# Row order of x, the first unit's y copied in place, the last token with its unit, later loads and a separate last gate in a fused recurrence and MLP

## The chip, the cores and the metric

One core of a Trainium2 chip runs the whole program. The metric is the device time of one execution in microseconds. All arithmetic is float32.

## The reference

A gated linear recurrence over 768 tokens for 4 batches and 8 heads of 48 channels, then an MLP with a quick GELU on its output:

```python
f = 1.0 / (1.0 + np.exp(-f_logit))                     # [4, 8, 768, 48]
for t in range(S):
    state = f[:, :, t, :, None] * state + np.einsum('bhd,bhe->bhde', k[:, :, t], v[:, :, t])
    y[:, :, t] = np.einsum('bhd,bhde->bhe', q[:, :, t], state)
x = y.transpose(0, 2, 1, 3).reshape(3072, 384)
h = x @ w_in                                           # w_in [384, 2048]
out = (h * (1.0 / (1.0 + np.exp(-1.702 * h)))) @ w_out  # w_out [2048, 384]
```

## The kernel before

**Units.** The 3072 tokens are 12 units of 256 (three to a batch; `NALL = 12`, `N_FILL = 3`). Each unit goes through an attention part (`attention(n)`) and an MLP part, and TensorE interleaves the MLP of earlier units (`fill`) with the attention of the next (`merge`). The order on TensorE and POOL is written out by hand throughout. Up to `fill_order.close()`, that is through the opening and `merge(1)` to `merge(3)`, the order on all engines is written by hand; behind that ScalarE, VectorE and SP are ordered by the framework. SP issues nearly all transfers, in one list; an instruction at its head that waits holds back what is behind it.

**Attention of a unit.** f, q and k are loaded into `raw` (`load_raw`), turned so that channels lie on partitions (`turn`: by TensorE through PSUM tiles t for units 0 to 2, by VectorE later), and worked through in six doubling levels: ScalarE sets keys aside (`Kc`, L494), TensorE makes scores (`sc`, L425), VectorE multiplies X by the gates (`promote`, L519 and L523) and moves scores into A (`evacuate`; L475 on ScalarE for the last level). The gates are products of f on POOL (`begin_gates`, L416): each level halves the row `tot`, and the last level goes to a tile of its own, `D64`, for units above 4. The states st of the four chunks are computed by VectorE from pd and the last gate (L667, L668). Tokens of the second half are kept in reverse order, so the rows of v for one half are reversed (`reverse_v`, a VectorE shuffle, L309). TensorE adds A times v (`add`, L534) and the states times q (L689) into y, a PSUM tile.

**From y to x.** y has 64 partitions for each of two groups of heads, of which 48 are used, and four pairs of heads a (`NP = 4`). ScalarE copies y to yT (L701, eight copies, 48 partitions by 256 columns) and SP moves it to xT, which has three tiles of 128 rows (`NK = 3`): three of the four pairs lie in rows 0 to 95, the fourth pair is split over rows 96 to 127 (`to_x`, L740 and L745; six transfers a unit). The rows of w_in are loaded in the same order. `half(0)` and `half(1)` do this for each half of the partitions. The last token's y (q is used one token late) is computed apart, behind the last unit (L724, L730, six more transfers).

**MLP.** Units 0 to 3 compute h directly from xT and w_in (L1087). From unit 4 on h is computed by 20 products in place of 24, on sums E of blocks of x that POOL makes (`sums_of_x`, L955) and sums of w_in blocks. The products of a unit follow a list, `WHOLE`, or for the last unit, which has two more columns and works in two column groups, `HALVES`: each item names a product, its group and a lane. Lanes 0 to 3 are PSUM tiles of their own; lanes 4 and 5 are the halves of one tile (h_y in the profile), 6 and 7 of another (h_sc). An item -1 emits four of the 16 matmuls that are still to do for the unit before (the last two products, o_Y and o_Z). The product with w_out takes seven products instead of eight (`mlp_o7`, L856).

**Weights.** 16 pairs of blocks of w_in and w_out are loaded as bits (`fetch_weights`, L210), rounded by ScalarE and VectorE (`begin_pair`, `convert`, L228 to L233) and written to w_in and w_out during units 0 to 3.

**Opening.** `opening()` loads unit 0, turns it, runs its six levels, turns its k (`turn_k`), evacuates, turns q and k of unit 1 and computes the states and y of unit 0. Just ahead of the states' end one element of y is copied onto itself by ScalarE (`seen`, L654).

Of the kernel before, what the change touches and what calls it, by code (L numbers as in the profile page):

```python
# [23 lines left out]
def kernel(  # L24
# [134 lines left out]
    def query(n, f):  # L159

        return ((2, 3), (4, 5) if n < N_FILL else (0, 5))[n % 2][f]

    q_end = const.tile([P, NP], F32, name="q_end")
    nc.gpsimd.memset(q_end, 0.0)

# [2 lines left out]
    w_in = const.tile([P, NK, DFF], F32, name="w_in")  # L168
    w_out = const.tile([P, NFF, DM], F32, name="w_out")
    k_toks = [tc.dram_tile([2, G, P // 32, 32 * NP], F32, name=f"k_tok{j}") for j in range(2)]  # L170
    D2, DR = 2 * D, P - 2 * D
    assert NP == NK + 1 and NK * DR == D2

    NGR = NFF // FG

# [2 lines left out]
    for r in range(NGR):  # L178
        ffs = range(r * FG, (r + 1) * FG)
        for ff in ffs[::2]:  # L180
            f = slice(ff * P, (ff + 2) * P)
            pairs.append((w_in[:, :, f], [
                (lambda t: t[:D2], moe_w_in[0:NK * D2, f].rearrange("(c p) f -> p c f", c=NK)),
                (lambda t: t[D2:], moe_w_in[NK * D2:DM, f].rearrange("(c p) f -> p c f", c=NK)),
            ]))
        for ff in ffs[::2]:
            pairs.append((w_out[:, ff:ff + 2, :], [
                (lambda t: t[:], moe_w_out[ff * P:(ff + 2) * P, :].rearrange("(c p) f -> p c f", c=2))]))
# [100 lines left out]
    def load_v(n):  # L289


        if n >= NALL:
            return
        b, s0 = n // NU, n % NU * U
        vts[n] = ld.tile([P, 2, DM], F32, tag="vt", name=f"vt_{n}", bufs=2)
        vrs[n] = ld.tile([P, DM], F32, tag="vr", name=f"vr_{n}", bufs=1)
        nc.sync.dma_start(
            out=vts[n][:, 1].rearrange("p (h d) -> p h d", h=H), in_=v[b, :, s0:s0 + HALF, :].rearrange("h p d -> p h d")
        )
        for i in range(4):  # L300
            t0 = s0 + U - 32 * (i + 1)
            nc.sync.dma_start(
                out=vrs[n][32 * i:32 * (i + 1)].rearrange("p (h d) -> p h d", h=H),
                in_=v[b, :, t0:t0 + 32, :].rearrange("h p d -> p h d"),
            )

    def reverse_v(n):

        nc.vector.stream_shuffle(vts[n][:, 0], vrs[n], list(range(31, -1, -1)))  # L309

    def rows(h):
# [7 lines left out]
    def attention(n):  # L319
# [86 lines left out]

        def begin_gates():
            t["tot"], off = att.tile([P, NA], F32, tag="tot", name=f"tot_{n}"), 0
            for m in LEV:
                nb = NA // (2 * m)  # L410
                t2 = t["tms"][-1].rearrange("p (n two) -> p n two", two=2)
                tn = t["tot"][:, off:off + nb]

                if m == LEV[-1] and n > N_FILL + 1:
                    tn = att.tile([P, nb], F32, tag="D64", name=f"D64_{n}", bufs=2)
                nc.gpsimd.tensor_tensor(tn, t2[:, :, 0], t2[:, :, 1], ALU.mult)  # L416
                t["tms"].append(tn)
                off += nb
# [212 lines left out]
        def _():  # L631
# [40 lines left out]
        def _():  # L672
# [4 lines left out]
            for cs in ((1, 0), (2, 3)):  # L677
                for a in range(NP):
                    for c in cs:
                        g, f = CHUNK[c]  # L680
                        w = HS
                        if t["before"][c] is None:
                            if not n:
                                continue
                            w = 1
                        for h in range(2):
                            state = t["before"][c][rows(h), a] if w > 1 else t["ahead"][rows(h), NC - 1, a]
                            x = a * HALF + g * HS
                            nc.tensor.matmul(  # L689
                                py[columns(h, g), g, a, f, :w], lhsT=state, rhs=X[rows(h), query(n, f), x:x + w],  # L690
                                start=False, stop=True, skip_group_check=True,
                            )
            yT = att.tile([P, NP, NG, G], F32, tag="kn", name=f"yT_{n}", bufs=1)
            xT = mlp.tile([P, NK, width(n)], F32, tag="xT", name=f"xT_{n}", bufs=3)
            if width(n) > U:
                nc.gpsimd.memset(xT[:, :, U + 1:], 0.0)
            def half(h):
                for f in (1, 0):
                    for g in range(NG):
                        at, step = (g * HS, 1) if f else (U - 1 - g * HS, -1)  # L700
                        nc.scalar.copy(view(yT[rows(h)], at, [[U, NP], [step, HS]]), py[columns(h, g), g, :, f, :])  # L701
# [14 lines left out]
            xTs[n] = xT  # L716
            if n == 0:
                fetch_weights()
            if n == NALL - 1:

                pl = ps.tile([P, NP], F32, tag="sc", name="y_last")
                for a in range(NP):
                    for h in range(2):
                        nc.tensor.matmul(  # L724
                            pl[rows(h), a:a + 1], lhsT=last["st"][rows(h), NC - 1, a], rhs=q_end[rows(h), a:a + 1],
                            start=True, stop=True,
                        )
                yl = att.tile([P, NP], F32, tag="q_last", name="yT_last", bufs=1)
                for h in range(2):
                    nc.scalar.copy(yl[rows(h)], pl[rows(h)])  # L730
                yl = yl.rearrange("p (a g t) -> p a g t", g=1, t=1)
                to_x(lambda h: (yl[rows(h), :NK], lambda r, d: yl[r:r + d, NK]), xT[:, :, U:U + 1], 1)
            if n > N_FILL:
                sums_of_x(n)

        def to_x(y, x, ng, hs=range(2)):

            for h in hs:
                most, rest = y(h)
                nc.sync.dma_start(out=x[h * D:(h + 1) * D].rearrange("p c (g t) -> p c g t", g=ng), in_=most)  # L740
                at = 0
                while at < D:
                    c, p = (h * D + at) // DR, (h * D + at) % DR
                    w = min(D - at, DR - p)
                    nc.sync.dma_start(  # L745
                        out=x[D2 + p:D2 + p + w, c].rearrange("p (g t) -> p g t", g=ng), in_=rest(h * HS + at, w)
                    )
                    at += w
# [53 lines left out]
    def mlp_o7(n, g):  # L802
# [77 lines left out]
    ))  # L880

    HALVES = tuple((x % 20 if x >= 0 else None, x // 20, lane) for x, lane in (
# [77 lines left out]
    def mlp_h20(n, g, before):  # L960
# [64 lines left out]
        def begin():  # L1025
# [231 lines left out]
    def opening():  # L1257
# [39 lines left out]
        begin_pair(1)  # L1297
# [61 lines left out]
```

## Time and profile before

| | |
|---|---|
| Median of 3 runs | 599.58 us (599.23 to 601.0) |
| The profiled execution | 599.25 us, span 597.1 us |
| TensorE (PE) busy | 575.8 us, 96% |
| VectorE (DVE) | 429.8 us, 72% |
| ScalarE (ACT) | 291.6 us, 49% |
| POOL | 136.6 us, 23% |
| Granted TensorE clock, mean | 0.994 |
| h<-xT,w_in (L1087) | 384 records, 388 ns mean |
| yT<-y (L701) | 96 copies, 366 ns mean |

A fp32 matmul shows as two records. PEld is the load of the stationary operand beside the matmul. "Idle before, releaser" says how long an engine stood still ahead of an instruction, and what ended the wait. A span is from the first instruction to the last; the execution's time has some 2 us more around it.

### The profile page before, as it was taken

The numbers are of one execution on the slowest core, as the hardware profiler recorded it, in microseconds if no ns is written. First come the engines' busy times: TensorE is split into PE (matmuls) and PEld (weight loads), VectorE is DVE, ScalarE is ACT, GpSimd is POOL, SyncE is SP. The second block draws the span as 40 slices with busy tenths as digits, with TensorE's granted clock in tenths as the row PEclk, the third lists the DMA queues.
The fourth block names the chain that finished last, engine by engine and source line by source line (L and its number), as shares of the span: only waits on it lengthen the run. The fifth ranks groups of instructions, "written<-read, shape, count | busy, mean of one in ns | idle before, by whom it ended". The sixth has DMA issues, their size and how long they took to land.

```text
span 597.1 us, 18468 instructions
## 1 busy us (share of the span) xinstructions
PE 575.8 (96%) x7814; PEld 514.1 (86%) x7814; DVE 429.8 (72%) x696; ACT 291.6 (49%) x613; POOL 136.6 (23%) x214
## 2 busy tenths in 40 slices
PE   7869899999999999999999999999999999999897
PEld 6746676867768689999999999999999999999897
DVE  2898987965766867889778789776887786361284
ACT  4655644453333352474475474574663564552440
POOL 3031110140026216420610600800700602203000
PEclk9979999999999999999999999999999999999999
DMA  7947867950143553253452343552362211001000
GB/s 187 208 111 184 191 153 185 242 112 1 41 105 74 142 127 69 73 134 88 116 152 55 81 112 91 135 133 59 91 161 49 63 37 29 27 3 26 28 1 26
DMA packets 83314, 58.29 MB, mean 98 GB/s; under 512 B 33633, under 2 KB 75265, under 8 KB 83233
## 3 DMA queue, kind: packets, MB, share of 16 engines
q1 hardware_dynamic: 82896, 56.73, 38.4%
q8 instruction: 61, 1.00, 0.8%
q10 hardware_dynamic: 337, 0.39, 0.3%
q14 instruction: 20, 0.16, 0.1%
HBM read 43.98 MB, written 8.39 MB: 88 GB/s over the span
## 4 chain that ended last, share of the span: by engine, by line
PE 87%; DVE 6%; ACT 3%; issue 2%; POOL 1%; DMA 1%; SPq 0%; DVEq 0%; ACTq 0%
PE h L993 17%; PE h L1087 13%; PE o_Y L856 11%; PE o L1101 10%; PE o_Z L856 7%; PE h_y L993 6%; PE sc L425 6%; PE o_W L856 4%; PE o_X L856 4%; PE t L357 2%; PE y L534 2%; PE y L689 2%; PE sc L643 1%; ACT yT L701 1%; DVE X L519 1%
## 5 line engine op out<-in xcount | busy, mean ns | idle before, releaser
L1087 PE MATMUL h<-xT,w_in 128*128 128x256 f32 x384 | 89.4, 388 | 1.9 <-DMA xT<-yT 1.9
L1087 PEld LDWEIGHTS h<-xT,w_in 128*128 128x128 f32 x384 | 72.8, 193 | 14.1 <-DMA xT<-yT 2.1
L523 DVE TENSOR_TENSOR X<-X,tot 128x1024 f32<-128x1024 f32 x45 | 57.0, 1266 | 37.9 <-PE sc L425 29.3
L494 ACT COPY Kc<-X 128x512 f32<-128x512 f32 x72 | 48.3, 671 | 67.7 <-DVE X L523 53.5
L1101 PE MATMUL o<-w_out,g 128*128 128x384 f32 x192 | 65.5, 491 | 0.4 <-DVE w_out L233 0.4
L955 POOL TENSOR_TENSOR E<-xT 128x128 f32<-128x128 f32 (+1 forms) x32 | 17.9, 569 | 206.6 <-DMA xT<-yT 97.3
L1101 PEld LDWEIGHTS o<-w_out,g 128*128 128x128 f32 x192 | 35.4, 190 | 22.7 <-DVE w_out L233 0.9
L993 PE MATMUL h<-E,w_in 128*128 128x128 f32 (+1 forms) x420 | 53.4, 275 | 0.0
L856 PE MATMUL o_Y<-T,S 128*128 128x192 f32 x288 | 50.6, 329 | 0.0
L993 PEld LDWEIGHTS h<-E,w_in 128*128 128x128 f32 x420 | 50.1, 192 | 0.0
L1023 ACT ACTIVATE g<-g 128x512 f32<-128x512 f32 (+1 forms) x63 | 35.6, 583 | 25.9 <-DVE g L1021 25.2
L1091 ACT ACTIVATE g<-h 128x256 f32<-128x256 f32 x64 | 23.8, 382 | 49.6 <-PE h L1087 49.2
L856 PEld LDWEIGHTS o_Y<-T,S 128*128 128x128 f32 x288 | 46.8, 190 | 0.5
L701 ACT COPY yT<-y 48x256 f32<-48x256 f32 x96 | 35.1, 366 | 21.7 <-PE y L689 20.6
L485 DVE COPY_PREDICATED A<-masks,sc 128x256 f32<-128x256 uint32 (+1 forms) x98 | 41.9, 504 | 0.1
L1021 DVE TENSOR_TENSOR g<-g,h 128x512 f32<-128x512 f32 (+1 forms) x52 | 31.7, 631 | 12.6 <-PE h L993 11.5
L372 POOL TENSOR_SCALAR F<-F 128x1024 f32<-128x1024 f32 x10 | 17.1, 1711 | 95.6 <-ACT F L375 83.8
L345 DVE STREAM_TRANSPOSE X<-raw 128x512 f32<-128x512 f32 x36 | 38.2, 1108 | 0.1
L425 PEld LDWEIGHTS sc<-X,Kc 48*64 48x64 f32 x1440 | 26.2, 136 | 11.1 <-ACT Kc L494 4.9
L425 PE MATMUL sc<-X,Kc 48*64 48x64 f32 x1440 | 30.9, 222 | 4.7 <-ACT Kc L494 1.9
L1021 DVE TENSOR_TENSOR g<-g,h_y 128x512 f32<-128x512 f32 (+1 forms) x26 | 16.5, 633 | 22.2 <-PE h_y L993 21.3
L1012 ACT ACTIVATE g<-h 128x512 f32<-128x512 f32 (+1 forms) x46 | 26.2, 578 | 10.0 <-PE h L993 9.8
(161 smaller groups left out, 1153.0 us busy)
## 6 DMA issues: line engine op xcount, KB each, us to landing
bits<-in_moe_w_out_dram SPq DMA_DIRECT2D x8, 768.0 KB, 6.9
raw<-in_f_logit_dram SPq DMA_DIRECT2D x48, 96.0 KB, 3.0
raw<-in_k_dram SPq DMA_DIRECT2D x48, 96.0 KB, 3.4
bits<-in_moe_w_in_dram SPq DMA_DIRECT2D x8, 576.0 KB
raw<-in_q_dram SPq DMA_DIRECT2D x44, 96.0 KB, 2.2
k_tok<-z SPq DMA_DIRECT2D x56, 64.0 KB, 1.8
kt<-k_tok SPq DMA_DIRECT2D x14, 256.0 KB, 3.2
xT<-yT SPq DMA_DIRECT2D x24, 144.0 KB, 2.6
```

The costliest lines, as they stand in the source:

```text
L345: nc.vector.transpose(view(out, at, [[HALF, NP], [step, R4], [R4 * step, 32]]), by_half[:, j, f].rearrange("p a (j d) -> p (a j) d", j=R4) ...
L425: nc.tensor.matmul(t["sc"][h][g * HS:(g + 1) * HS, a, s, :], lhsT=t["Kc", l][rows(h), x:x + HS], rhs=rhs(h, a, g), start=True, stop=True,)
L485: moved = nc.vector.copy_predicated(out=view(A, c * HALF + at, dims), mask=mask.bitcast(U32), data=got)
L494: nc.scalar.copy(c.rearrange("p (n two m) -> p n two m", two=2, m=m), view(X, KF * SLOT, [[2 * m, SLOT // (2 * m)], [(KR - KF) * SLOT + m, ...
L523: nc.vector.tensor_tensor(x, x, y, ALU.mult)
L701: nc.scalar.copy(view(yT[rows(h)], at, [[U, NP], [step, HS]]), py[columns(h, g), g, :, f, :])
L856: nc.tensor.matmul(t[name], lhsT=lhs(f), rhs=rhs(f), start=(new and i == 0), stop=(i == HF - 1), skip_group_check=True,)
L993: nc.tensor.matmul(ph[:, t], lhsT=WA[a][:, f * P:(f + 1) * P], rhs=E[n][b], start=(root and t == 0), stop=not goes_on, skip_group_check=True,)
L1021: nc.vector.tensor_tensor(to, to, part, ALU.add if sign > 0 else ALU.subtract)
L1023: nc.scalar.activation(to, to, AF.Gelu_apprx_sigmoid)
L1087: nc.tensor.matmul(ph, lhsT=w_in[:, c, ff * P:(ff + 1) * P], rhs=xTs[n][:, c, :], start=(c == 0), stop=(c == NK - 1))
L1101: nc.tensor.matmul(t["po"], lhsT=g[ff // FG][:, ff % FG, tt * P:(tt + 1) * P], rhs=w_out[:, ff, :], start=(ff == ffs[0]), stop=(ff == ffs[ ...
```

## The change

Five things are changed together.

- x and w_in take their rows in the order of y's partitions: rows 0 to 47 and 64 to 111 of a tile hold three of the four pairs of heads, rows 48 to 63 and 112 to 127 the fourth. A unit's y goes to x in eight transfers, a w_in pair is loaded in four.
- For unit 0, ScalarE copies the three pairs straight from y into xT; only the fourth pair goes through yT and six small transfers, and its copies come first. The rows of v for unit 0 are loaded in one transfer and reversed by a matmul with a reversed identity, `turned`. Unit 1's first `Kc` is emitted behind `seen`.
- For the last unit, `whole` computes the last token's y ahead of the copies, puts it into yT as a 257th column, and moves both in eight transfers.
- The third pair of weights and unit 2's f are loaded behind unit 1's v.
- `D64` has its own tile from unit 4 on (before: from 5), and the list `HALVES` and the assignment of lanes to PSUM tiles in the last unit are changed.

```diff
+    turned = const.tile([P, P], F32, name="turned")
+    nc.gpsimd.memset(turned, 0.0)
+    nc.gpsimd.affine_select(
+        out=turned, in_=turned, compare_op=ALU.not_equal, fill=1.0, base=1 - P, pattern=[[1, P]], channel_multiplier=1
+    )
...
-    D2, DR = 2 * D, P - 2 * D
-    assert NP == NK + 1 and NK * DR == D2
+    D2, DR = 2 * D, HS - D
+    assert NP == NK + 1 and NK * DR == D
...
-                (lambda t: t[:D2], moe_w_in[0:NK * D2, f].rearrange("(c p) f -> p c f", c=NK)),
-                (lambda t: t[D2:], moe_w_in[NK * D2:DM, f].rearrange("(c p) f -> p c f", c=NK)),
+                (lambda t, h=h: t[h * HS:h * HS + D], moe_w_in[0:NK * D2, f].rearrange("(c h p) f -> h p c f", c=NK, h=2)[h])
+                for h in range(2)
+            ] + [
+                (lambda t, h=h: t[h * HS + D:(h + 1) * HS],
+                 moe_w_in[NK * D2:DM, f].rearrange("(h c p) f -> h p c f", c=NK, h=2)[h])
+                for h in range(2)
...
     def load_v(n):
...
+        if n == 0:
+            nc.sync.dma_start(
+                out=vrs[n].rearrange("p (h d) -> p h d", h=H), in_=v[b, :, s0 + HALF:s0 + U, :].rearrange("h p d -> p h d")
+            )
+            return
...
     def reverse_v(n):
 
+        if n == 0:
+            pt = bank([P, DM], f"v_{n}")
+            nc.tensor.matmul(pt, lhsT=turned, rhs=vrs[n], start=True, stop=True)
+            nc.scalar.copy(vts[n][:, 0], pt)
+            return
...
-            if n >= N_FILL or (n == 1 and R - 4 in pieces):
+            if n >= N_FILL:
                 load_raw(n + 1, 0)
...
             else:
+                if between:
+                    between()
                 set_aside(0)
...
-                if m == LEV[-1] and n > N_FILL + 1:
+                if m == LEV[-1] and n > N_FILL:
                     tn = att.tile([P, nb], F32, tag="D64", name=f"D64_{n}", bufs=2)
...
             if not n:
-                units[1][0][2]()
-                add()
-
-                seen = t["py"][HS:HS + 1, 1, 0, 1, :1]
-                nc.scalar.copy(seen, seen)
+                def values():
+                    add()
+
+                    seen = t["py"][HS:HS + 1, 1, 0, 1, :1]
+                    nc.scalar.copy(seen, seen)
+                units[1][0][2](values)
             load_v(n + 1)
+            if not n:
+                fetch_weights()
+                load_raw(2, 0)
...
+            if n == NALL - 1:
+                whole(py)
+                return
...
+            def copies(h, to, heads):
+                for f in (1, 0):
+                    for g in range(NG):
+                        at, step = (g * HS, 1) if f else (U - 1 - g * HS, -1)
+                        nc.scalar.copy(
+                            view(to, at, [[U, heads.stop - heads.start], [step, HS]]), py[columns(h, g), g, heads, f, :]
+                        )
+
             def half(h):
+                if n == 0:
+                    copies(h, yT[rows(h), NK:], slice(NK, NP))
+                    to_x(lambda h: (None, lambda r, d: yT[r:r + d, NK]), xT[:, :, :U], NG, (h,))
+                    for x in (0, 1) if h else ():
+                        copies(x, xT[rows(x)], slice(0, NK))
+                    return
...
+        def whole(py):
+
+            w = width(n)
+            yT = att.tile([P, NP, 1, w], F32, tag="kn", name=f"yT_{n}", bufs=1)
...
+            for h in range(2):
+                for f in (1, 0):
+                    for g in range(NG):
+                        at, step = (g * HS, 1) if f else (U - 1 - g * HS, -1)
+                        nc.scalar.copy(view(yT[rows(h)], at, [[w, NP], [step, HS]]), py[columns(h, g), g, :, f, :])
+                nc.scalar.copy(yT[rows(h), :, 0, U], pl[rows(h)])
+                to_x(
+                    lambda h: (yT[rows(h), :NK, :, :U + 1], lambda r, d: yT[r:r + d, NK, :, :U + 1]), xT[:, :, :U + 1], 1, (h,)
+                )
...
         def to_x(y, x, ng, hs=range(2)):
...
-                nc.sync.dma_start(out=x[h * D:(h + 1) * D].rearrange("p c (g t) -> p c g t", g=ng), in_=most)
...
+                if most is not None:
+                    nc.sync.dma_start(out=x[rows(h)].rearrange("p c (g t) -> p c g t", g=ng), in_=most)
+                for c in range(NK):
                     nc.sync.dma_start(
-                        out=x[D2 + p:D2 + p + w, c].rearrange("p (g t) -> p g t", g=ng), in_=rest(h * HS + at, w)
+                        out=x[h * HS + D:(h + 1) * HS, c].rearrange("p (g t) -> p g t", g=ng),
+                        in_=rest(h * HS + c * DR, DR),
                     )
...
-        (38, 1), (-1, -1), (0, 6), (37, 4), (-1, -1), (-1, -1), (39, 4), (-1, -1), (34, 5), (2, 7),
-        (15, 6), (30, 4), (33, 1), (22, 0), (18, 3), (1, 7), (20, 2), (25, 5), (32, 4), (24, 1),
+        (38, 1), (-1, -1), (0, 6), (37, 4), (-1, -1), (39, 4), (34, 5), (2, 7), (-1, -1),
+        (15, 6), (30, 4), (33, 1), (22, 0), (18, 3), (-1, -1), (1, 7), (20, 2), (25, 5), (32, 4), (24, 1),
...
-            lanes["h"] = [free[x] for x in (1, 2, 0, 3)]
+            lanes["h"] = [free[x] for x in ((1, 2, 0, 3) if groups == 1 else (1, 2, 3, 0))]
...
         fetch_weights()
-        fetch_weights()
         for l in range(NL):
...
-        chosen[:] = [2, 3]
+        chosen[:] = [2, 3, 2]
+        units[0][3]()
         turn_k(0)
         turn_k(2)
         for l in range(NL - 1):
             evacuate(l)
-            if l == 1:
-                units[0][3]()
```

`chosen` lists the PSUM banks that the next tiles take; `units[0][3]` is `reverse_v(0)`, and `units[1][0][2]` is unit 1's `begin_k`.

More of the change, by code (lines that the diff above doesn't have):

```diff
@@ L692, in _ @@
                             )
+            if n == NALL - 1:
+                whole(py)
+                return
             yT = att.tile([P, NP, NG, G], F32, tag="kn", name=f"yT_{n}", bufs=1)
             xT = mlp.tile([P, NK, width(n)], F32, tag="xT", name=f"xT_{n}", bufs=3)
-            if width(n) > U:
-                nc.gpsimd.memset(xT[:, :, U + 1:], 0.0)
-            def half(h):
+            def copies(h, to, heads):
[5 more added lines that the diff above has]
+                        )
+            def half(h):
+                if n == 0:
[4 more added lines that the diff above has]
+                    return
                 for f in (1, 0):
@@ L718, in _ @@
                 fetch_weights()
[L719 to L732, printed above, removed]
             if n > N_FILL:
                 sums_of_x(n)
+        def whole(py):
+            w = width(n)
+            yT = att.tile([P, NP, 1, w], F32, tag="kn", name=f"yT_{n}", bufs=1)
+            xT = mlp.tile([P, NK, w], F32, tag="xT", name=f"xT_{n}", bufs=3)
+            nc.gpsimd.memset(xT[:, :, U + 1:], 0.0)
+            pl = ps.tile([P, NP], F32, tag="sc", name="y_last")
+            for a in range(NP):
+                for h in range(2):
+                    nc.tensor.matmul(
+                        pl[rows(h), a:a + 1], lhsT=last["st"][rows(h), NC - 1, a], rhs=q_end[rows(h), a:a + 1],
+                        start=True, stop=True,
+                    )
+            for h in range(2):
+                for f in (1, 0):
[5 more added lines that the diff above has]
+                    lambda h: (yT[rows(h), :NK, :, :U + 1], lambda r, d: yT[r:r + d, NK, :, :U + 1]), xT[:, :, :U + 1], 1, (h,)
+                )
+            xTs[n] = xT
+            sums_of_x(n)
         def to_x(y, x, ng, hs=range(2)):
@@ L739, in to_x @@
                 most, rest = y(h)
[L740 to L744, printed above, removed]
+                if most is not None:
+                    nc.sync.dma_start(out=x[rows(h)].rearrange("p c (g t) -> p c g t", g=ng), in_=most)
+                for c in range(NK):
                     nc.sync.dma_start(
-                        out=x[D2 + p:D2 + p + w, c].rearrange("p (g t) -> p g t", g=ng), in_=rest(h * HS + at, w)
+                        out=x[h * HS + D:(h + 1) * HS, c].rearrange("p (g t) -> p g t", g=ng),
+                        in_=rest(h * HS + c * DR, DR),
                     )
-                    at += w
         return (begin_f, begin, begin_k, begin_gates), parts, (open_level, open_evacuate, turn_k), lambda: reverse_v(n)
```

## The prediction

> **What bounds the kernel now.** I read the page's forty slices first, then the chain of waits, then the timeline where a slice is not full. The slices say where time can be won at all:
>
> ```profile
> PE   7869899999999999999999999999999999999897
> ...
> PEclk9979999999999999999999999999999999999999
> ```
>
> TensorE is full from about 76 us to 547 us: there, work that other engines gain or lose is free unless it makes TensorE wait. In windows of 10 us between 160 and 550 it is short of full in two stretches only, 230 to 250 (0.74 us) and 530 to 540. So the sum is made in three places: the opening, one wait at 244 us, the end.
>
> The opening, from the timeline (start, length, engine, line, operation, and in brackets the idle time ahead and its releaser):
>
> ```profile
> 33.60 3.02 ACT L701 COPY yT<-y 48x256 f32<-48x256 f32 x8 [1.29 <-PE y L689]
> ...
> 35.13 0.61 SPq L740 DMA_DIRECT2D xT<-yT  x1
> ...
> 36.65 0.69 ACT L494 COPY Kc<-X 128x512 f32<-128x512 f32 x1
> ...
> 37.10 0.53 SPq L740 DMA_DIRECT2D xT<-yT  x1
> 37.39 0.95 PEld L425 LDWEIGHTS sc<-X,Kc 48*64 48x64 f32 x32 [2.08 <-ACT Kc L494]
> ...
> 37.68 1.86 SPq L745 DMA_DIRECT2D xT<-yT  x2
> ...
> 40.45 2.07 PE L1087 MATMUL h<-xT,w_in 128*128 128x256 f32 x4 [1.93 <-DMA xT<-yT]
> ```
>
> See ScalarE copying y for 3.02 us, SP issuing six transfers one behind the other, and TensorE idle twice: until Kc, queued behind the copies, and until xT. The stretches of half a microsecond (busy time by engine, then the granted clock)[...]:
>
> ```profile
> 37.50:38.00 0.50, 0.50 (x22) 0.50 (x26) 0.47 (x2) 0.00 (x0) 0.00 (x0) 0.50 0.19 45
> ...
> 43.50:44.00 0.50, 0.50 (x2) 0.35 (x2) 0.47 (x2) 0.30 (x1) 0.00 (x0) 0.50 1.05 375
> ...
> 44.50:45.00 0.50, 0.50 (x4) 0.17 (x2) 0.50 (x2) 0.00 (x0) 0.00 (x0) 1.00 1.15 289
> ```
>
> Half clock from 37.2 to 44.0, so the first 12 h matmuls take 4.61 us and the next 12 take 2.86. The chain then runs on VectorE without a break from 47.65 (released by the score matmuls that follow those h) to 71.5, and TensorE is full from 76. Hence what the first h gain, everything behind gains, until VectorE itself is the limit: it idles 2.51 us before 47.65.
>
> At 244 us the chain goes back to a gate:
>
> ```profile
> 235.30 1.04 POOL L416 TENSOR_TENSOR tot<-F 128x512 f32<-128x512 f32 x1 [3.33 <-DVE st L667]
> ...
> 238.85 0.36 DVE L667 TENSOR_TENSOR st<-st,D 128x192 f32<-128x192 f32 x1 [1.97 <-POOL D L416]
> ...
> 244.14 0.69 PE L425 MATMUL sc<-Qc,Kc 48*64 48x64 f32 x32 [0.52 <-ACT osb L830]
> ```
>
> POOL waits for st(4) to let go of tot, VectorE waits for POOL's D, and the promotes and copies behind end 0.68 us after TensorE is ready (o_Z ends at 243.46).
>
> At the end, three products waited for an engine that read the other half of their shared PSUM tile (h_y or h_sc); the first:
>
> ```profile
> 554.53 0.61 PE L993 MATMUL h_sc<-E,w_in 128*128 128x129 f32 x4
> ...
> 555.18 0.39 ACT L1012 ACTIVATE g<-h_sc 128x258 f32<-128x258 f32 x1
> 555.62 0.71 PE L993 MATMUL h_sc<-xT,N_p 128*128 128x129 f32 x4 [0.48 <-ACT g L1012]
> ```
>
> The product at 554.53 (item 2 of the list, lane 7) is read at 555.18, and the next one (15, lane 6) starts 0.04 us after that. Each such hole costs its wait and 0.26 us of refill (0.71 against 0.45).
>
> [...] L793 took 1.67 us beside POOL's L917 at 226.28, and 0.69 alone.
>
> **The change, part by part.**
>
> *Reversal of the first v by TensorE.* Added behind the last score (22.71): one 128x384 matmul, 0.73 us by the row of o_last (same width), and a copy, 0.48 by L1151. Removed from VectorE at 25.13: a shuffle, 0.69. The matmul takes bank 2, the first turn_k bank 3, the second bank 2 again: it waits for the v copy (23.44 + 0.03 + 0.48 = 23.95), ends near 24.6, its kn copy near 25.2. The q transposes then start at 25.2, not 23.98; but before they stood 0.80 us at 24.41 on "issue", which this wait now covers (price without that cover: 0.8). So pd ends at 28.3 instead of 28.09. The y sums start behind ScalarE's A copies: q copies to 28.05, weights 0.92, A 1.49, that is 30.5; before, 29.98 and a stop of 0.82 on "issue". They end at 32.1, about as now. VectorE gains nothing: its st chain waits for pd.
>
> *y straight into x.* The fit through 366 ns for 256 columns and 156 for 4 (L730) gives 206 ns for 64 and 313 for 192. ScalarE: 8 x 0.215 + 8 x 0.32 = 4.3 us instead of 3.02. From 33.55 the small copies of the first half end at 34.4, of the second at 35.3, all at 37.8; Kc follows to 38.5, 1.2 late, and the scores behind it, 1.13 at half clock, end at 39.7. SP: six transfers as before, all small; three from 34.45, three more, at 0.6 each, the last issued at 37.45. In the trace the last was issued at 38.3 and the data was there 2.1 later; so xT is complete at 39.55. First h at 39.7: **0.75 earlier**. The clock: if it returns at 44.0 as now, most of that is lost again (0.3 left)[...]; I take **-1.0**, bounds -2.1 and +0.8 (the stop of 0.8 not covered).
>
> *Kc behind "seen"*: ScalarE waits there anyway (0.17 before 32.20), and Kc ends at 33.1, when its scores come. Nothing; uncovered 0.4. *Loads later*: vr(1), one w_out pair and f(2), 1.4 MB, are queued on SP behind vr(1)'s wait for the new matmul (23.45) instead of a shuffle at 25.8; DMA moves 170 to 290 GB/s there, so they end near 31, ahead of the xT transfers at 34.4; the pair is wanted at 40.3. Nothing; if they came into the xT transfers, up to 1. *w_in in four transfers a pair*: 2 x 0.41 on SP at 6.2, where SP next waits for TensorE until 8.73. Nothing. *turned on POOL*: 0.5 us by ident's rows at 3.2; POOL is next wanted at 9.47. Nothing.
>
> *Units 1 to 10, xT in 8 transfers instead of 6*: +1.2 us of SP a unit, its loads, k_tok and stores behind it, POOL's E sums 0.6 to 1.2 later. Unit 5: E ready from 289.4 on, first h20 product 293.74, the second needs the fourth sum (292) at 295.81. Unit 1: xT there at 80.4, wanted at 82.0. **0**, bounds 0 and +5 (below).
>
> *D64 apart for unit 4.* POOL is free at 231.98, so the gates of unit 5 end at 235.3, not 238.8; VectorE's 1.97 us of waiting and TensorE's 0.68 go. Against it, the gates now run beside the st chain (232.93 to 235.6), on whose end scores at 235.76 wait[...]. I take **-0.4**; bounds -0.7 and +0.7.
>
> *Order of the end.* With HALVES' new order, product 15 and product 1 (holes of 0.74 and 0.71 at 555.1 and 558.1) get a block of o_Y or o_Z (1.30 us) ahead of them. But 34 now follows 39 directly in the other lane of h_y: by the rule above it waits 0.63 and 0.26. And 20 starts on Z's bank, 0.2 to 0.4 for VectorE's L816. -1.45 + 0.9 + 0.2 = **-0.4**, bounds -1.4 and +0.5. *Last token with the last unit*: 8 transfers instead of 12, E sums 2.4 us earlier; but no product here waited for them. Nothing; it is only cover.
>
> Sum: -1.0 - 0.4 - 0.4 = -1.8 on the profiled execution's 599.25 (span 597.1), which is 0.33 below the median: **597.4**.
>
> **Rivals.**
> [...]
> *ScalarE takes the place of the transfers.* 1.3 us more of copies ahead of Kc, and cold scores behind: the first h gains nothing, gates or end about 0.4: 598.9. For it: Kc's wait (1.58) is already there. Chance 0.18.
> *Slower: SP's list.* Two more transfers a unit move the raw loads, k_tok and kt; from unit 3 on the order on ScalarE, VectorE and SP is not written by hand, so scores may come to wait for Kc as at 244, 0.74 a time, in the seven units behind: +5.2 - 1.8 = 602.6. It turns the sign from the third unit, and counts as slower from the fifth. Against it: slacks of 1.6 to 3 us above. For it: VectorE is 90% busy in many windows. Chance 0.20.
> *My forecast*: 0.42, itself 596.6 to 598.4.
>
> **How the numbers follow.** A measurement can tell 0.3%, 1.8 us: below 597.8 is faster. My forecast lies below it five times in six (0.35 of 0.42), with the clock rival's 0.20: faster 0.55. Same: 0.07 and 0.18. Slower: 0.20. The range 595.4 to 600.6 takes in both bounds of the opening and three late units, and leaves out most of the SP rival.
>
> **What would show it.** First h near 39.7; half clock shorter; TensorE full from about 75; no wait of POOL on st near 235 nor of scores near 243; a new hole at the fourth product of the last unit and none at 15 and 1. Scores waiting for Kc in units 5 to 11, or a first h behind 40.5, would prove me wrong.

## The result, and the profile after

The kernel after takes 602.27 us (median of 11 runs, 599.27 to 606.61), the kernel before 599.23 (11 runs beside it); the ratio is 1.0049, 95% interval 1.0032 to 1.0066. So the change makes the kernel slower, by more than the 0.3% that can be told from no change, where I forecast 597.4. The profiled execution took 601.40 us, span 599.6.

The slices of the page after, to be held against those of before:

```profile
PE   7978999989999999999999999999999999999997
...
PEclk9979999999999999999999999999999999999999
```

Behind the opening only the ninth slice (120 to 135 us) is short of full where before it was not. A coarse view hides the rest, so I went through the trace product by product: the **shift** of a moment is the start of a product of TensorE in this trace less the start of the same product in the trace before (the added v matmul left out). Each trace is one execution.

| us | 20 | 44 | 56 | 76 to 100 | 112 | 120 to 128 | 136 to 220 | 260 to 548 | 560 to the end |
|---|---|---|---|---|---|---|---|---|---|
| shift | -0.87 | -2.04 | -1.80 | -1.32 | +0.53 | +0.90 | +2.79 | +2.27 | +1.88 |

Read it as a ledger: TensorE is ahead up to 100 us, 4.6 us are lost between 56 and 136 us, the gate gives 0.5 and the end 0.4. The first entry, -0.87 at 20 us, stands ahead of any copy of y.

The opening after, from the timeline (start, length, engine, line, operation, idle time and its releaser):

```profile
32.10 1.88 ACT L729 COPY yT<-y 48x64 f32<-48x64 f32 x8 [0.49 <-PE y L715]
...
33.12 3.76 SPq L796 DMA_DIRECT2D xT<-yT  x6
34.00 2.58 ACT L729 COPY xT<-y 48x192 f32<-48x192 f32 x8
36.61 0.69 ACT L516 COPY Kc<-X 128x512 f32<-128x512 f32 x1
...
38.42 4.84 PE L1138 MATMUL h<-xT,w_in 128*128 128x256 f32 x12
```

The small copies come first, the six transfers go out beside the large copies, and the first h starts at 38.42 instead of 40.45, with no wait of its own. Half clock still lasts 6.8 us (35.6 to 42.5; before, 37.2 to 44.0), as the stretches of half a microsecond show (last columns: granted clock, DMA share, GB/s):

```profile
35.50:36.00 0.50, 0.00 (x0) 0.00 (x0) 0.50 (x2) 0.48 (x3) 0.00 (x0) 0.65 0.14 33
...
42.00:42.50 0.50, 0.50 (x3) 0.41 (x2) 0.50 (x1) 0.00 (x0) 0.00 (x0) 0.53 0.93 212
```

The gate and the end, from the timeline:

```profile
234.74 1.49 POOL L438 TENSOR_TENSOR tot<-F 128x512 f32<-128x512 f32 x1
...
246.41 0.69 PE L447 MATMUL sc<-Qc,Kc 48*64 48x64 f32 x32
```

```profile
554.46 0.71 PE L1044 MATMUL h_y<-xT,w_in 128*128 128x129 f32 x4 [0.53 <-ACT g L1063]
555.00 0.61 PE L1044 MATMUL h_sc<-E,w_in 128*128 128x129 f32 x4
555.45 1.47 PE L907 MATMUL o_Z<-w_out,g 128*128 128x192 f32 x8
...
556.75 0.61 PE L1044 MATMUL h_sc<-xT,N_p 128*128 128x129 f32 x4
```

POOL no longer waits for st, nor do the scores for Kc. Product 34 has the new hole (0.53), and product 15 at 556.75 has none, because a block of o_Z stands ahead of it.

The loss, first before, then after: the w_out pair that ScalarE converts near 103 us, the turn of k behind it, and unit 2's first h. In the trace before:

```profile
97.44 0.39 SPq L210 DMA_DIRECT2D bits<-in_moe_w_out_dram  x1
...
102.26 0.90 ACT L228 ACTIVATE a<-bits 128x768 f32<-128x768 f32 x1 [0.70 <-DMA bits<-in_moe_w_out_dram]
...
108.87 0.60 PE L595 MATMUL tkn<-ident,X 128*128 128x128 f32 x4
...
129.40 0.53 SPq L740 DMA_DIRECT2D xT<-yT  x1
...
132.17 5.20 PE L1087 MATMUL h<-xT,w_in 128*128 128x256 f32 x22
```

And after:

```profile
98.88 0.38 SPq L220 DMA_DIRECT2D bits<-in_moe_w_out_dram  x1
...
103.66 0.92 ACT L238 ACTIVATE a<-bits 128x768 f32<-128x768 f32 x1 [3.42 <-DMA bits<-in_moe_w_out_dram]
...
104.61 0.56 DVE L240 TENSOR_SCALAR s<-a 128x768 int32<-128x768 int32 x1 [4.30 <-ACT a L238]
...
109.35 0.66 PE L617 MATMUL tkn<-ident,X 128*128 128x128 f32 x4 [1.35 <-DVE sum L1204]
...
132.84 1.85 SPq L796 DMA_DIRECT2D xT<-yT  x3
...
135.13 2.24 PE L1138 MATMUL h<-xT,w_in 128*128 128x256 f32 x9 [1.97 <-DVE sum L1204]
```

SP issues the pair 1.44 us later although TensorE stands 1.32 earlier. It takes 4.8 us to land in both traces, so ScalarE waits 3.42 instead of 0.70, VectorE behind it 4.30, and TensorE stops for VectorE's sums. At 135 TensorE stops again. The view puts that to a sum, but in the program this h also waits for the transfers that fill xT's first tile: the last of them is the fourth of six before (issued at 129.40, 2.77 us ahead of the h), the sixth of eight after (132.84, 2.29 us ahead of it). So before had some 0.5 us to spare there.

SP's own waits between 60 and 136 us (who waited for whom, us in total, times, longest), first before, then after, show what its list stood behind:

```profile
SPq L278 <- DVE F L345: 5.5, 1, 5.5
SPq L278 <- DMA bits<-in_moe_w_out_dram: 3.1, 2, 1.9
```

```profile
SPq L288 <- DMA bits<-in_moe_w_out_dram: 4.6, 2, 2.9
SPq L288 <- DMA bits<-in_moe_w_in_dram: 3.6, 5, 1.3
...
SPq L288 <- DVE F L365: 1.8, 1, 1.8
SPq L317 <- DMA bits<-in_moe_w_in_dram: 1.6, 2, 1.3
```

Before, SP had 5.5 us to spare in front of one load; after, that slack is 1.8, and SP waits 5.2 us for pieces of w_in to land, which it never did before. The counters that the traces name at each issue say why it waits for them at all: the transfers of SP and ScalarE raise eight counters in turn (526 issues before, 555 after, out of turn in one place), and 307 and 345 of the issues wait on the very counter that they raise, that of the transfer eight places ahead. After's two pairs of w_in, issued from 61.95 to 66.49, take all eight; the transfer of v at 67.75, eight places behind the piece of 62.31, then waits for w_in, and so does that at 71.65, eight behind the piece of 65.17. The list stands still while its head waits: loads of f go out every 0.47 us or so up to 82.92, the next, which waits for a w_out pair, at 85.14, and those of q only behind it, from 85.54.

### The profile page after: what moved, and what is told of

Same layout as the page of the kernel before. It is cut to its first block, busy times and chain, and to the rows that moved or that the text cites. A ratio compares the mean times of both kernels' runs of the same rounds, so it can differ in the third digit from the quotient of the medians.

```text
span 599.6 us, 18541 instructions
## 1 busy us (share of the span) xinstructions
PE 576.4 (96%) x7816; PEld 514.0 (86%) x7816; DVE 429.2 (72%) x694; ACT 293.6 (49%) x622; POOL 137.3 (23%) x216
## 4 chain that ended last, share of the span: by engine, by line
PE 79%; DVE 9%; DMA 4%; SPq 3%; issue 2%; ACT 2%; POOL 1%; DVEq 0%; ACTq 0%
PE h L1044 17%; PE o_Y L907 11%; PE h L1138 10%; PE o_Z L907 8%; PE h_y L1044 6%; PE o L1152 6%; PE sc L447 6%; PE o_X L907 4%; PE o_W L907 4%; PE t L377 2%; DMA bits<-in_moe_w_in_dram 2%; PE y L715 1%; PE y L556 1%; PE sc L665 1%; DVE X L541 1%
## 5 line engine op out<-in xcount | busy, mean ns | idle before, releaser
L743 ACT COPY yT<-y 48x256 f32<-48x256 f32 x80 | 29.3, 366 | 17.4 <-PE y L715 16.4
```

## The experiments

The runs first take parts of the change away or try them alone (e1 to e8, e11, e12), then ask whether the number of w_in's transfers or their shape costs (e9, e10), and then test the shape (e13 to e16).

**First theory: the number of transfers.** SP's list, by issue time and by the eight places, is late in the stretches behind units 1 and 2. Rivals: the eight transfers of xT alone, or the moved loads. Four kernels take each number alone. "Shift" below is what a kernel loses between 56 and 136 us against before, by its one trace; after itself loses 4.59.

*e1_after_w2*, w_in in two transfers again:

```diff
-  (t[h * HS:h * HS + D] ...) for h in range(2)] + [(t[h * HS + D:(h + 1) * HS] ...) for h in range(2)
+  (t[:2 * D], ...), (t[2 * D:], ...)
```

> The changed kernel, but each w_in pair comes in two transfers (96 and 32 rows, as before) instead of four; the rows of w_in then do not fit those of x, so its output is not the reference's. Theory 1 (SP's list is late because every transfer waits for the landing of the one eight places ahead of it, and the w_in pairs now take four of the eight places each): w_out's pair at 99 us and unit 2's x at 133 us come in time again, TensorE gets back most of the 4.2 us that it lost between 100 and 136 us: 598 to 599 us. Theory 2 (the two more transfers of a unit's y do it): no better than 601. Theory 3 (the loads that were moved later do it): 602.

598.66 us, ratio 1.000 (0.9984 to 1.0016), shift 1.43. Going back to two transfers a pair regains 3.6 us by the medians, 3.2 by the traces and 2.9 by the ratios: the largest single part of the loss.

*e2_after_x6*, six transfers of y a unit:

```diff
+                if most is not None:
+                    nc.sync.dma_start(
+                        out=x[h * HS + D:(h + 1) * HS, :2].rearrange("p c (g t) -> p c g t", g=ng), in_=y(h)[0][:DR, :2]
+                    )
                 for c in range(NK):
+                    if most is not None and c < 2:
+                        continue
```

> The changed kernel, but y of units 1 to 11 goes to x in six transfers instead of eight (the fourth pair's first two pieces are replaced by one transfer of as many bytes from other rows, so the output is not the reference's). Theory 1: little, at most 1 us of the 4.2, since xT(1) has 1.6 us to spare: 601 to 602. Theory 2: 598 to 599. Theory 3: 602.

600.66 us, ratio 1.0025 (1.0011 to 1.0039), shift 3.98. It regains 1.6 us by the medians, 1.4 by the ratios and 0.6 by the traces, so whether it is more than the 1 us that I gave it is open.

*e3_before_w4*, the kernel before with four transfers a pair (48, 48, 16, 16 partitions):

```diff
-  (t[:D2], ...), (t[D2:], ...)
+  (t[h * D:(h + 1) * D], ...) for h in range(2), (t[D2 + h * 16:D2 + (h + 1) * 16], ...) for h in range(2)
```

> The kernel before, with the same rows, but each w_in pair split into four transfers (48, 48, 16, 16 rows). Theory 1: the loss alone, without the change's gains: 602 to 604, with TensorE waiting near 104 and 132 us. Theory 2 and 3: 599 to 600.

600.65 us, ratio 1.0029 (1.0017 to 1.0041), shift 1.12. Alone it costs less than within the change (3.2 by the traces), where less slack is left; but its pieces also lie on other partitions (0 to 47, 48 to 95, 96 to 111, 112 to 127, where after has 0 to 47, 64 to 111, 48 to 63, 112 to 127), which may matter: a packet of w_in near 63 us takes 171 ns here and 197 in after.

*e4_before_x8*, the kernel before with eight transfers a unit:

```diff
-                    w = min(D - at, DR - p)
+                    w = min(D - at, DR - p, 16)
```

> The kernel before, but y goes to x in eight transfers a unit (the 32-row piece split in two). Theory 1: 599.5 to 600.5 (0.6 us of SP's time in the opening, and no more). Theory 2: 602 to 603. Theory 3: 599.

603.65 us, ratio 1.0080 (1.0054 to 1.0105): 4.4 us by the medians (6 runs), and the trace shows two losses: 1.97 up to 136 us, 1.45 of it at unit 2's first h, and 2.2 at the last unit, where the last token's transfers (eight instead of six here) stand behind xT's. Its timeline:

```profile
547.65 1.86 SPq L745 DMA_DIRECT2D xT<-yT_last  x3
...
551.06 0.78 POOL L955 TENSOR_TENSOR E<-xT 128x129 f32<-128x129 f32 x2 [20.34 <-DMA xT<-yT_last]
...
551.52 0.71 PE L993 MATMUL h<-E,N_c 128*128 128x129 f32 x4 [1.95 <-POOL E L955]
```

The second loss is not in after, because `whole` moves the last token with its unit. Both changes to the transfers cost, then; it remained to show what the rest of the change is worth.

**The parts apart.** *e5_after_both*, after with the edits of e1 and e2 (the diffs of both).

> The kernel after with both increases in transfers taken back: each pair of w_in in two transfers (96 and 32 partitions) and y into x in six for units 1 to 11, whole last unit included; the rows of w_in and x do not agree, so its output is not the reference's. Theory 1 (the transfers are the whole loss: SP's list runs late in the two stretches behind units 1 and 2, and each transfer waits for the landing of the one eight places ahead): the offset of TensorE's records to the kernel before stays at -1.0 or below through 104 to 136 us, and the gate (-0.6) and the end (-0.4) come on top: 597.4 to 598.2, ratio 0.997 to 0.9985. Theory 2 (the moved loads, or the data of the weights themselves, hold the two stretches where they were, however early the opening ends): the offset returns to 0 or above near 104 or 132 us, and 598.2 to 599.3 remain.

597.68 us, ratio 0.9984 (0.9963 to 1.0005), shift 0.42. The two changes to the transfers are nearly the whole loss; without them the change is worth 1.8 us by the medians and 1.0 by the ratio, whose interval just reaches no difference.

*e6_gate_end*, the kernel before with `n > N_FILL` at D64, HALVES and its lanes as in after:

```diff
-                if m == LEV[-1] and n > N_FILL + 1:
+                if m == LEV[-1] and n > N_FILL:
```

> The kernel before with two parts of the change alone: the last gates apart (D64) from unit 4 on, and the order of the last unit's list with its PSUM tiles. Theory 1: the wait of POOL for st near 235 us goes (-0.6) and the end gains 0.4, nothing is lost: 598.2, ratio 0.998 to 0.999. Theory 2 (what the trace of after shows at these places is a shift by the late stretches, and is not there when nothing runs late): no difference, 599.2.

598.35 us, ratio 0.9982 (0.9969 to 0.9995). In its trace the gate gives 0.51 and the end 0.39, about the 1.0 that theory 1 said, whatever runs late elsewhere.

*e7_opening*, the opening (with the later loads and the last token) on the old rows, where only the upper half of y can go straight into x:

```diff
+                if n == 0 and h == 0:
+                    copies(h, yT[rows(h), NK:], slice(NK, NP))
+                    to_x(lambda h: (None, lambda r, d: yT[r:r + d, NK]), xT[:, :, :U], NG, (h,))
+                    return
...
             half(1)
...
+                copies(0, xT[:D], slice(0, NK))
```

> The kernel before with the opening of the change alone, on the old rows: v of unit 0 turned by TensorE, the Kc turn ahead of the second copy of the state, gates earlier, one pair of weights and f of unit 2 loaded later, the last token with the last unit; and of unit 0's y the upper half copied straight into x (its rows 0 to 47 are the same in y and in x), the lower half by transfers as before, so five transfers stand in the opening where there were six, and all other units keep six and w_in its two. Theory 1: the first h comes 0.7 to 1.2 sooner and nothing behind takes it back: 598.0 to 598.6. Theory 2 (the weights' data hold the stretch behind unit 1: the w_out pair that is wanted near 102 us): what is gained above 0.9 is lost there and at 132 us, 598.6 to 599.3.

597.71 us, ratio 0.9979 (0.9965 to 0.9993). In its trace half clock lasts 3.4 us, 37.5 to 40.9, instead of 6.8: the sooner end that the clock rival counted on. But e7 gains as much without it. The trace's mean clock is 0.997, where that of before, with 6.8 us at half clock, has 0.994; of e7's 22 executions 6 have 0.997 and 13 have 0.994, with medians of 597.65 and 597.68 us.

*e12_opening_no_copy*, e7 without that copy (the diff above taken out):

> The kernel of e7_opening without the copy into x: all of unit 0's y through yT and six transfers as before; what is left of the opening are v by TensorE, the Kc turn ahead, the gates earlier, the loads later and the last token with the last unit. Theory 1 (the copy straight into x makes the gain of e7_opening, 1.2 to 1.8 us): 598.8 to 599.6. Theory 2 (the other parts cover the stops on issue and make it): 597.6 to 598.2.

598.64 us, ratio 1.0000 (0.9985 to 1.0016). By the two ratios the copy makes the opening's gain, about 1.3 us (0.9 by the medians), though the two intervals together leave it anywhere from nothing to 2.5; v by TensorE, the order of Kc and the gates, the last token and the later loads make none that can be told.

*e8_best*, e7 and e6 together:

> The opening of e7_opening and the gates and end of e6_gate_end together. Theory 1: the sum, -0.7 to -1.2 and -1.0: 597.2 to 597.7. Theory 2: the gates and the end alone, 598.2.

597.33 us, ratio 0.9968 (0.9952 to 0.9985), shift -0.18: faster than before, and than after.

*e11_best_early_loads*, e8 with the loads in their old place:

```diff
-            if not n:
-                fetch_weights()
-                load_raw(2, 0)
...
+        fetch_weights()                       # in opening()
```

> The kernel of e8_best with the loads where they were before: the second further pair of weights in the opening's first list, f of unit 2 behind the second half of unit 1's decay. Theory 1 (the moved loads are neutral, as the prediction had it): 597.0 to 597.8, as e8_best. Theory 2 (the moved loads fall into the stretch in which TensorE runs short of instructions, and cause its stops on issue between 24 and 35 us): 0.5 to 1.0 less, and a narrower spread. A third outcome, slower by 0.5 or more, would say that the loads in their early place hold up the first v and Kc.

597.27 us, ratio 0.9975 (0.9962 to 0.9987), as e8 within both intervals. The moved loads are neutral. What does vary from execution to execution is the opening: in the profiled execution of e5, TensorE stopped 1.39 us on "issue" at 32.21; after's trace has no such stop in the same work.

**Second theory: is it the number?** *e9_two_and_two_small* keeps after's count with the weights in two pieces:

```diff
             engine.dma_start(out=part(by_dst), in_=src.bitcast(I32))
+        for i in range(2) if len(parts) == 2 else ():
+            engine.dma_start(out=small[2 * n + i:2 * n + i + 1], in_=parts[0][1].bitcast(I32)[:1, 0, :16])
```

> The kernel of e1_after_w2 (after, each pair of w_in in two transfers of 96 and 32 partitions; its rows do not agree with x, so its output is not the reference's), with two more transfers of 64 bytes each behind every pair of w_in, into a tile of their own: as many transfers on SP's list as in after, but the weights in pieces as before. Theory 1 (the number counts: issue time on SP, and places that a later transfer has to wait for): most of what after loses to e1_after_w2 comes back, 600.5 to 602.5. Theory 2 (the shape counts: pieces of 48 and 16 partitions land later than those of 96 and 32): 598.3 to 599.3, as e1_after_w2.

599.13 us, ratio 0.9998 (0.9985 to 1.0010), shift 1.40, both as e1. My first theory falls here as far as w_in goes: two transfers more a pair on SP's list, and in the eight places, cost nothing that can be told. SP even waits 6.6 us for w_in in this trace, so the length of that wait does not tell what is lost.

*e10_after_pool_queue*, after with the two 16-partition pieces issued by GpSimd:

```diff
-            engine.dma_start(out=part(by_dst), in_=src.bitcast(I32))
+            (nc.gpsimd if i > 1 and n > 2 else engine).dma_start(out=part(by_dst), in_=src.bitcast(I32))
```

> The kernel after, with the two smaller of the four transfers of a pair of w_in issued by GpSimd instead of SP from the fourth pair of weights on: the same pieces, the same rows, two transfers fewer on SP's list and among those that wait for the one eight places ahead. Theory 1 (SP's list and the places are the loss): 598.5 to 600.0, near e1_after_w2. Theory 2 (the shape of the pieces is the loss): as after, 601.5 to 603. A third outcome, over 603, would say that GpSimd's own issue makes the gates or the sums of E late.

602.95 us, ratio 1.0060 (1.0038 to 1.0082): nothing gained. It weighs little by itself, since its w_out pair took 6.6 us to land (issued 100.61, used 107.20) where before and after took 4.8, and behind TensorE's stop of 1.89 us there eight h records take 2.70 us (108.65), where after has ten in 2.32 (109.84); the trace's mean clock is 0.991, after's 0.994.

What do the transfers move? In the first 10 us from the pairs of w_in near 63 us (forty slots of 0.25 us), before and after have

```profile
DMA packets 2875, 1.97 MB, mean 197 GB/s; under 512 B 2106, under 2 KB 2106, under 8 KB 2874
...
q1 hardware_dynamic: 2874, 1.95, 92.5%
```

```profile
GB/s 0 0 0 16 66 90 246 385 287 164 139 164 172 205 188 131 156 164 147 164 229 164 123 156 147 115 213 156 147 148 156 156 164 246 139 139 164 156 139 168
DMA packets 854, 1.53 MB, mean 153 GB/s; under 512 B 116, under 2 KB 116, under 8 KB 853
...
q1 hardware_dynamic: 853, 1.51, 92.4%
```

and e9 has 193 GB/s. The DMA engines are equally busy (last column), yet move less. These stretches hold other transfers too, in different shares; the packets of w_in alone say the same. The two pairs are 768 packets of 2 KB in each trace, and one takes 134 ns on average before, 141 in e9 and 197 after (from the packet times in the traces). In the two other groups of two pairs behind 40 us it is 130 and 135, 133 and 136, 174 and 179. **The pieces themselves are slow.** What sets them apart is how many partitions a piece covers: 96 and 32 before and in e9, 48 and 16 after. That this sets the rate, and the GB/s that the expectations below give with it, were my estimate. Three kernels test it.

*e13_before_w4_columns*, four transfers again, but cut along the chunks, so that each keeps the old partitions:

```diff
+                (lambda t, p=p, c=c: t[p, c], rows[:, c])
+                for p, rows in ((slice(0, D2), ...), (slice(D2, P), ...)) for c in (slice(0, 2), slice(2, NK))
```

> The kernel before with each pair of w_in in four transfers, as many as in e3_before_w4, but cut along the chunks and not along the partitions: 96 partitions with two chunks and with one, 32 partitions with two and with one. Theory A (the partitions that a transfer reaches set its rate[...]): no loss against before, 599.2, ratio 0.9985 to 1.0015, and about 190 GB/s in the 10 us from the first transfer near 63 us, as in before (197). Theory B (four transfers a pair cost by their number): 600.3 to 601, as e3_before_w4, and 150 to 165 GB/s.

598.27 us, ratio 0.9991 (0.9978 to 1.0004), shift -0.25. Against e3, with the same count and the same bytes in the same kernel, the DMA view reads, e3 first:

```profile
GB/s 0 0 0 8 147 156 303 385 229 164 156 147 156 279 279 230 238 123 164 205 148 188 115 172 205 180 148 131 131 172 197 295 238 229 191 164 118 92 127 133
DMA packets 1421, 1.69 MB, mean 169 GB/s; under 512 B 655, under 2 KB 655, under 8 KB 1420
```

```profile
GB/s 0 0 0 0 66 98 180 295 352 377 344 287 254 295 262 139 148 131 123 213 262 385 352 279 270 311 254 295 182 183 191 201 200 221 210 190 115 151 72 76
DMA packets 2982, 1.99 MB, mean 199 GB/s; under 512 B 2212, under 2 KB 2212, under 8 KB 2980
```

While w_in arrives, e13 moves 250 to 385 GB/s in most slots, e3 115 to 280; a packet of w_in takes 118 ns in e13 and 171 in e3 (in the other two groups 120 and 129, 166 and 177). The number of pieces is the same, and their sizes overlap (64 to 384 KB in e13, 96 to 288 in e3). So the number is cleared, and it is the cut along the partitions that makes them slow.

*e14_before_w2_halves*, two transfers of 64 and 64 partitions:

```diff
-  (t[:D2], ...), (t[D2:], ...)
+  (t[h * HS:(h + 1) * HS], ...) for h in range(2)
```

> The kernel before with each pair of w_in in two transfers, as many as before, but of 64 and 64 partitions instead of 96 and 32 (the rows of w_in and x do not agree then, so its output is not the reference's). Theory A: [...] 165 to 185 GB/s in the 10 us from the first transfer near 63 us, and half the loss of e3_before_w4, 599.6 to 600.1. Theory B (the number alone): as before, 197 GB/s and 599.2.

186 GB/s and 146 ns a packet, between before (197 and 134) and e3 (169 and 171), a little above what I expected in GB/s; 599.13 us, ratio 0.9999 (0.9982 to 1.0015). The trace loses 1.58, the medians nothing: the time is inconclusive.

*e15_after_two_queues*, after with the pieces of partitions 64 to 127 issued by GpSimd:

```diff
+            (nc.gpsimd if i % 2 and n > 2 else engine).dma_start(out=part(by_dst), in_=src.bitcast(I32))
```

> The kernel after, with the pieces of each pair of w_in that lie in partitions 64 to 127 issued by GpSimd and those in 0 to 63 by SP, from the fourth pair of weights on. Theory A: [...] side by side they move more: 190 GB/s or more in the 10 us from the first transfer near 63 us, where e10_after_pool_queue had 155, and, if GpSimd's own issue costs nothing, 599 to 600.5. Theory B (the pieces are slow for another reason): 145 to 165 GB/s and 602 to 603, as after and e10_after_pool_queue.

605.44 us (4 runs), ratio 1.0103 (1.0069 to 1.0137), and 166 GB/s, not 190: theory A's expectation was missed. The w_out pair took 9.5 us to land (issued 99.82, used 109.30), TensorE stopped 4.79 us for it, the first h record behind the stop took 0.80 us (110.74; the longest at half clock in the opening before is 0.79), and the trace's mean clock is 0.989, so the time tells little of the pieces. Whether the pieces themselves or GpSimd's way of issuing hold it, these runs don't say; the verdict on partitions rests on e3 against e13 and on e9, all in SP's queue (171 ns a packet against 118 and 141), and why pieces on few partitions are slow is not shown.

*e16_best_columns*, e8 with e13's four transfers:

> The kernel of e8_best with w_in's pairs in four transfers cut along the chunks, as in e13_before_w4_columns. If the narrow partitions alone make the pieces slow, four transfers cost nothing here either: 596.8 to 597.5, ratio 0.9955 to 0.997, and ScalarE's wait for the w_out pair near 101 us (0.96 in e8_best) is gone as it is in e13. If the number costs after all, 598 or more.

596.45 us, ratio 0.9958 (0.9941 to 0.9975): the lowest here, 0.4% under before (its interval overlaps that of e8), with four transfers a pair. Of ScalarE's wait for the w_out pair 0.19 is left, where before waited 0.70 and after 3.42 (from its timeline):

```profile
98.98 0.90 ACT L236 ACTIVATE a<-bits 128x768 f32<-128x768 f32 x1 [0.19 <-DMA bits<-in_moe_w_out_dram]
```

## Why the prediction was wrong

**w_in in four transfers, "Nothing": the step that failed.** I priced SP's issue at the first pair, 2 x 0.41 us, and took the transfers themselves as unchanged because their bytes are. They are not: cut into 48 and 16 partitions a packet of w_in takes 197 ns where it took 134, and the pairs hold up what stands behind them (153 GB/s where there were 197). The term is worth 2.9 to 3.6 us within the change (e1), not nothing.

**Units 1 to 10, "0, bounds 0 and +5": a second term that was mis-sized.** I tested units 1 and 5, and not unit 2, whose first h has some 0.5 us to spare. Eight transfers cost 1.97 up to there (e4), inside my bounds; the value was wrong. Whether their number does it or their width (pieces of 16 rows where there were 32) was not tested. The two terms that I set at nothing are worth 1.12 (e3) and 1.97 (e4) alone by the traces, and 4.59 together, more than their sum. Two reasons offer themselves, and no run parts them: each uses up slack which the other needs, and after's pieces are slower than e3's near 63 us (197 ns a packet against 171; 174 to 179 against 166 to 177 in the other two groups).

**Opening, -1.0.** The chain was right, the size is in good part luck. From ScalarE's first copy to the first h I had 6.15 us (33.55 to 39.7), and the trace has 6.32 (32.10 to 38.42). But the copies began 1.45 us earlier than I said, in a trace in which TensorE's stops on "issue" in the opening sum to 0.3 us, where that of before has 2.5; these change from execution to execution. Half clock lasted 6.8 us as before, the case for which I had 0.3 left; the bound of -2.1 was my estimate of a sooner end, which no trace of before showed. Of the -1.32 at 76 us, 0.87 was there at 20 us; in between the trace gains 0.45. This opening, with both halves copied, was not run alone; for the copy of one half e7 against e12 gives 0.9 to 1.3. That TensorE is full from about 75 held.

**Gates, -0.4; end, -0.4.** Measured -0.5 and -0.4. The wait of POOL on st is gone and the hole moved from 15 to 34, as said.

**Loads later, "Nothing"**: right (e11). **Last token, "only cover"**: right, and worth more than I gave it: the 2.2 us that e4 loses at the last unit do not appear in after.

**Rivals.** *Slower: SP's list* had 602.6, nearly the result, by luck: it put the loss in units 5 to 11 at scores waiting for Kc, 0.74 each; the trace shows none there (the shift stands at +2.27 from 260 to 548), and e9 shows that two more transfers of weights a pair on SP's list cost nothing that can be told (599.13 us against 598.66 in e1). SP's list is still the likely reason for what the eight transfers of xT lose, but at unit 2. *The clock rival* (chance 0.20), that half clock ends sooner, was an estimate of mine; it did not come in after (6.8 us), and where it came, in e7 (3.4), it made no difference to the medians (597.65 and 597.68). *ScalarE takes the place of the transfers*: refuted, the first h waited for nothing.

My chances also leaned on a wrong reading of slack: a gain in the opening makes everything behind want its data earlier, so a term set at nothing had to be tested against the kernel as it would be after the gain, with 1.3 us less of cover.

## What to carry to other kernels

A transfer cut into pieces with the same bytes is not the same transfer: cut it along the free dimension and keep the partitions wide (four pieces cost nothing that can be told in e13, and 1.4 us in e3). Where a layout makes two engines' work cheaper, price what it does to every transfer that must follow the same rows, at the place where the queue has least slack. And find that place by walking the list to each consumer (here unit 2's first h), not by a sample of units.

## What the hardware showed that I had not expected

The busy share of the DMA engines doesn't show a slow transfer: at 92% busy they moved 197 GB/s before and 153 after; the mean time of a packet of one size shows it (134 and 197 ns). And two executions of one kernel differ by more than most of these edits are worth: after ran from 599.27 to 606.61 us, e8 from 595.23 to 601.41, with TensorE's stops on "issue" in the opening summing to 0.3 us in one trace (after) and 2.7 in another (e5). The mean clock goes with it in part: of after's 11 executions the three with a mean clock of 0.990 have a median of 604.42 us, the seven with 0.994 one of 601.40.
